# A gated linear attention with a max-out layer: one run of row-tiled products per unit, and two PSUM pairs that swap roles

## Chip, core and metric

The kernel runs on one core of one Trainium2 chip. The metric is the device time of the whole kernel in microseconds; the kernel before took 144.9 us (median of three runs, 144.42 to 144.99).

## The reference

Two stages, with B = 4 batches, H = 8 heads, S = 768 tokens, D = 48, a model width of 384 and 1024 hidden columns:

```python
# stage 1: a recurrence over the tokens, for each batch and head
for t in range(S):
    state = alpha[:, :, t, :, None] * state + np.einsum('bhd,bhe->bhde', k[:, :, t], v[:, :, t])
    y[:, :, t] = np.einsum('bhd,bhde->bhe', q[:, :, t], state)
# stage 2: on x = y as 3072 rows of H * D = 384
h1 = x @ w1
h2 = x @ w2
out = maximum(h1, h2) @ w_out
```

The kernel doesn't walk token by token. It takes chunks of 128 tokens, sums the logarithms of alpha along a chunk with matrix products, scales q and k by exponentials of those sums, and gets y as a masked product P = q k^T on v within the chunk plus q on the state at the chunk's start. The maximum is written as relu(x (w1 - w2)) + x w2, and the part that is linear in x uses w2 @ w_out, worked out once.

## The kernel before

A unit `u` is 256 tokens (two chunks, `cc` = 0 and 1) of one batch; there are NU = 12 units, in three rounds over the four batches (B = 4). In the step for `u` the attention of `u`, the max-out layer of `u - 1` and the beginning of `u + 1` are interleaved. The order of the statements is each engine's order of work (the schedule is a manual one), and every semaphore follows from which tiles an instruction reads and writes.

PSUM has eight banks here: `g0` to `g3` (one each), a pair `pp` and a pair `m`.

The pieces that matter, with cuts marked:

```python
def sumd(u):                       # decay sums of whole half chunks
    X = st[u]
    lg = X["lg"]
    cs = [new(f"g{i}", [128, 512], FP32, 1, "cs") for i in range(2)]
    X["csv"] = csv = [x[:, 0 : H * D]... for x in cs]          # cut
    X["dps"] = dps = cs[0][:, H * D : H * D + 4 * HP]...       # cut: other columns of the first bank
    for hp in range(HP):           # HP = 4 head pairs
        for j in range(2):
            nc.tensor.matmul(dps[:, hp], lhsT=pair(lg[:, j], hp), rhs=halves, ...)

def sumc(u):                       # running sums, one bank for each chunk; 64 rows each
    for j in range(2):
        for i in range(2):
            ...
                r = slice(64 * i, 64 * i + 64)
                m, x = mc[r, j], lg[r, j, :, 0:D]
            nc.tensor.matmul(csv[i], lhsT=m, rhs=x, start=(j == 0), stop=(j == 1))

def expm(u, cc):                   # ScalarE: Em = exp(-sum)
    nc.scalar.activation(out=Em, in_=X["csv"][cc], func=ACTF.Exp, scale=-1.0)
def expp(u, cc):                   # ScalarE: exp(sum), in place in PSUM
    nc.scalar.activation(out=X["csv"][cc], in_=X["csv"][cc], func=ACTF.Exp)
def expd(u):                       # ScalarE: de = exp(decay sums)
    nc.scalar.activation(out=X["de"], in_=X["dps"], func=ACTF.Exp)

def qmul(u, cc):                   # VectorE: qn = q * exp(sum)
    nc.vector.tensor_mul(out=X["qn"][cc][:, :, 0:D], in0=part(u, "qf", cc), in1=X["csv"][cc])

def kvmm(u, cc):                   # TensorE: k^T v of a chunk, into g3 or g2
    X["kvp", cc] = kvp = new(f"g{3 - cc}", [128, HP, 2 * D], FP32, 1, "kv")
    ...
def kvsum(u, cc): ...              # VectorE: tm = kv + scaled state, two instructions
def state(u, cc): ...              # GpSimd: sb = decayed state, from tm

def pmm(u, cc):                    # TensorE: P of a chunk; 48 rows, the two halves a at rows 0 and 64
    X["pa", cc] = pa = [new("pp", [128, HP, C], FP32, 2, "pp") for _ in range(2)]
    for j in range(HP):
        for a in range(2):
            r = slice(64 * a, 64 * a + D)
            nc.tensor.matmul(pa[a][:, j, :], lhsT=qk[r, 1, j, :], rhs=qk[r, 0, j, :], ...)
def pmask(u, cc, heads=(0, 1)): ...  # VectorE: pt = P * triangular mask, one instruction a half

def ystate(u):                     # TensorE: q on the state, begins Y; 48 rows
    X["ya"] = ya = [new(f"g{2 + a}", [128, 2, HP, D], FP32, 1, "ya") for a in range(2)]
    ...
def yin(u): ...                    # TensorE: pt on v, ends Y; ScalarE copies ya to xn
def xturn(u): ...                  # TensorE turns xn, into g2; VectorE copies to xt

def hid(u, f2, on_act=None, tag="m"):  # TensorE: six products; then relu on ScalarE or VectorE
    hp = new(tag, [128, 2, 2 * C], FP32, 2, "hp")
    ...
def outx(u, n): ...                # TensorE: three products into a new tile of "m"
def outg(u, n, ...): ...           # eight more onto it, then a copy on ScalarE
```

The step of the loop, for units 3 to 11 (the conditions of unit 2 are cut):

```python
for u in range(2, NU):
    nxt = u + 1 < NU
    ...
    kvmm(u, 0)
    pmm(u, 0)
    kvsum(u, 0)
    pmask(u, 0)
    state(u, 1)
    if more(u):                    # u + 4 < NU
        kvmm(u, 1)
    hid(u - 1, 0)
    hid(u - 1, 1)
    if nxt:
        sumd(u + 1)
    hid(u - 1, 2)
    if nxt:
        sumc(u + 1)
        expm(u + 1, 0)
        expp(u + 1, 0)
        expm(u + 1, 1)
    if more(u):
        kvsum(u, 1)
    pmm(u, 1)
    ystate(u)
    pmask(u, 1)
    hid(u - 1, 3, True)
    if nxt:
        expp(u + 1, 1)
        expd(u + 1)
        for cc in range(2):
            kmul(u + 1, cc)        # GpSimd: kn = k * Em
            qmul(u + 1, cc)
        state(u + 1, 0)
    outp(u - 1, 0)                 # outx and outg
    yin(u)
    if nxt:
        turn(u + 1, 0)             # kn and qn turned, into g0 and g1; VectorE copies to qk
        turn(u + 1, 1)
    outx(u - 1, 1)
    ...                            # xturn(u), v of u + 1, logarithms of u + 2, outg(u - 1, 1)
```

Of the kernel before, what the change touches and what calls it, by code (L numbers as in the profile page):

```python
# [9 lines left out]
FP32 = mybir.dt.float32  # L10
# [5 lines left out]
def kernel(  # L16
# [28 lines left out]
    B, H, S, D = q.shape  # L45
    C = 128
    HP = H // 2
    P64 = 64
    ND2 = S // (2 * C)
    NU = B * ND2  # L50
    NT, DM = out.shape
# [12 lines left out]
    nc.scalar.preload_act_table_set("natural_log_exp_and_others")  # L64

    st = {}

    def rows(src, u, lo, n):
        d, b = divmod(u, B)
        return src[b, :, d * 2 * C + lo : d * 2 * C + lo + n, :]  # L70
# [29 lines left out]
    def load(u):  # L100
        load_a(u)
        if u in PAIRED:
            load_fat(u, "kf", k)
            load_fat(u, "qf", q)
        else:
            load_kq(u, 0)
            load_kq(u, 1)
        load_v(u)
# [8 lines left out]
    for n in range(2):  # L117
        f = slice(n * NF // 2, (n + 1) * NF // 2)
# [4 lines left out]
    for n in range(4):  # L123
        f = slice(n * DFF // 4, (n + 1) * DFF // 4)
# [32 lines left out]
    for n in range(NB):  # L157
        t = constp.tile([128, 2, H, P64], FP16, name=f"lg{n}")
# [13 lines left out]
    for n in range(2 * NB):  # L172
        for lst, nm in ((QN, "qn"), (KN, "kn")):
            t = constp.tile([128, H, P64], FP16, name=f"{nm}{n}")
# [9 lines left out]
    def pair(t, j):  # L184
        return t[:, 2 * j : 2 * j + 2, :].rearrange("p h w -> p (h w)")

    def new(tag, shape, dtype, bufs, name):
        return psp.tile(shape, dtype, tag=tag, bufs=bufs, name=name)
# [21 lines left out]
                    nc.gpsimd.tensor_copy(out=X["v16"][64 * cc : 64 * cc + 64, 2], in_=i)  # L210

    def sums(u):
        sumd(u)
        sumc(u)

    def sumd(u):
        X = st[u]
        lg = X["lg"]
        cs = [new(f"g{i}", [128, 512], FP32, 1, "cs") for i in range(2)]
        X["csv"] = csv = [x[:, 0 : H * D].rearrange("p (h d) -> p h d", h=H) for x in cs]  # L220
        X["dps"] = dps = cs[0][:, H * D : H * D + 4 * HP].rearrange("p (j b n) -> p j b n", j=HP, b=2)
        for hp in range(HP):
            for j in range(2):
                nc.tensor.matmul(
                    dps[:, hp], lhsT=pair(lg[:, j], hp), rhs=halves, start=(j == 0), stop=(j == 1)
                )
# [100 lines left out]
    def kvsum(u, cc):  # L327
        X = st[u]
        tm = X[f"tm{cc}"] = gp.tile([128, HP, D], FP32, tag=f"tm{cc}", bufs=6 if cc else 3, name="tm")
        kvp = X["kvp", cc]  # L330
        for a in range(2):
            r = slice(64 * a, 64 * a + 64)
            e = slice(D * a, D * a + D)
            if ("sb", cc) in X:
                nc.vector.tensor_add(out=tm[r], in0=kvp[r, :, e], in1=X["sb", cc][r])  # L335
            else:
                nc.vector.tensor_copy(out=tm[r], in_=kvp[r, :, e])

    def more(u):
        return u + B < NU  # L340

    def pmm(u, cc):
        X = st[u]
        qk = X["qk"][:, cc].rearrange("p (n h) t -> p n h t", n=2)
        X["pa", cc] = pa = [new("pp", [128, HP, C], FP32, 2, "pp") for _ in range(2)]
        for j in range(HP):
            for a in range(2):
                r = slice(64 * a, 64 * a + D)
                nc.tensor.matmul(pa[a][:, j, :], lhsT=qk[r, 1, j, :], rhs=qk[r, 0, j, :], start=True, stop=True)  # L349

    def pmask(u, cc, heads=(0, 1)):
        X = st[u]
        if 0 in heads:
            X["pt", cc] = gp.tile([128, 2, HP, C], FP16, tag="pt", name="pt")
        pt = X["pt", cc]
        for a in heads:
            nc.vector.tensor_mul(  # L357
                out=pt[:, a], in0=X["pa", cc][a], in1=um.unsqueeze(1).to_broadcast([128, HP, C])
            )
# [4 lines left out]

    def ystate(u):
        X = st[u]
        X["ya"] = ya = [new(f"g{2 + a}", [128, 2, HP, D], FP32, 1, "ya") for a in range(2)]
        X["begun"] = begun = set()
        for cc in range(2):
            if ("sb", cc) not in X:  # L370
                continue
# [3 lines that stand above are left out]
                    nc.tensor.matmul(  # L375
                        ya[a][:, cc, j, :], lhsT=X["qk"][r, cc, j, :], rhs=X["sb", cc][r, j, :],
                        start=a not in begun, stop=False,
                    )
                    begun.add(a)
# [24 lines left out]
        X["xt"] = mp.tile([128, ND, 2, C], FP16, tag="xt", bufs=3, name="xt")  # L404
        nc.vector.tensor_copy(out=X["xt"], in_=xp)

    def hid(u, f2, on_act=None, tag="m"):
        X = st[u]
        if f2 == 0:
            X["gT"] = mp.tile([128, NF, 2 * C], FP16, tag="gT", name="gT")  # L410
        gT = X["gT"]
        hp = new(tag, [128, 2, 2 * C], FP32, 2, "hp")
        for n in range(2):
            f = 2 * f2 + n
            for ds in range(ND):
                nc.tensor.matmul(  # L416
                    hp[:, n, :], lhsT=w12[:, ds, f * 128 : (f + 1) * 128],
                    rhs=X["xt"][:, ds].rearrange("p n t -> p (n t)"), start=(ds == 0), stop=(ds == ND - 1),
                )
        if f2 != 3 if on_act is None else on_act:  # L420
            nc.scalar.activation(out=gT[:, 2 * f2 : 2 * f2 + 2, :], in_=hp, func=ACTF.Relu)  # L421
        else:
            nc.vector.tensor_relu(out=gT[:, 2 * f2 : 2 * f2 + 2, :], in_=hp)
# [5 lines left out]
    def outx(u, n):  # L429
        X = st[u]  # L430
        if n == 0:
            X["outs"] = mp.tile([128, 2, DM], FP32, tag="outs", bufs=4, name="outs")
        X["op"] = op = new("m", [128, DM], FP32, 2, "op")
        for ds in range(ND):
            nc.tensor.matmul(op, lhsT=X["xt"][:, ds, n, :], rhs=w2o[:, ds, :], start=(ds == 0), stop=False)  # L435

# [14 lines left out]
    def dst(u):  # L451
        d, b = divmod(u, B)
        t0 = b * S + d * 2 * C
        return out[t0 : t0 + 2 * C, :].rearrange("(p j) d -> p j d", j=2)

    def outlast(u, n):

        X = st[u]
        for e in range(2):
            c = slice(e * 2 * DM // 3, DM if e else 2 * DM // 3)  # L460
            op = new("m", [128, c.stop - c.start], FP32, 2, "oq")
            for ds in range(ND):
                nc.tensor.matmul(op, lhsT=X["xt"][:, ds, n, :], rhs=w2o[:, ds, c], start=(ds == 0), stop=False)
            for f in range(NF):
                nc.tensor.matmul(
                    op, lhsT=X["gT"][:, f, n * C : (n + 1) * C], rhs=wo16[:, f, c], start=False, stop=(f == NF - 1)
                )
            if e == 0:
                nc.scalar.copy(out=X["outs"][:, n, c], in_=op)
                nc.scalar.dma_start(out=dst(u)[:, n, c], in_=X["outs"][:, n, c])  # L470
            else:
                nc.vector.tensor_copy(out=X["outs"][:, n, c], in_=op)
                nc.sync.dma_start(out=dst(u)[:, n, c], in_=X["outs"][:, n, c])
# [141 lines left out]
    for u in range(2, NU):  # L615
        nxt = u + 1 < NU
        if u + 4 < NU:
            load(u + 4)
        if u == 2:
            pmm(u, 0)  # L620
            pmask(u, 0)
            hid(u - 1, 0)
        kvmm(u, 0)
        if u > 2:
            pmm(u, 0)
        kvsum(u, 0)
        if u > 2:
            pmask(u, 0)
        state(u, 1)
        if more(u):  # L630
            kvmm(u, 1)
        if u > 2:
            hid(u - 1, 0)
        hid(u - 1, 1)
        if nxt:
            sumd(u + 1)
        hid(u - 1, 2)
        if nxt:
            sumc(u + 1)
            expm(u + 1, 0)  # L640
            expp(u + 1, 0)
            expm(u + 1, 1)
        if more(u):
            kvsum(u, 1)
        pmm(u, 1)
        ystate(u)
        pmask(u, 1)
        hid(u - 1, 3, True)
        if nxt:
            expp(u + 1, 1)  # L650
            expd(u + 1)
            for cc in range(2):
                kmul(u + 1, cc)
                qmul(u + 1, cc)
            state(u + 1, 0)
        outp(u - 1, 0)
        yin(u)
        if nxt:
            turn(u + 1, 0)
# [3 lines that stand above are left out]
            xturn(u)  # L663
            vcast(u + 1)
            if u + 2 < NU:
                ln(u + 2)
            outg(u - 1, 1)
        else:
            outg(u - 1, 1, (0, 1, 2, 3))
            xturn(u)  # L670
            outg(u - 1, 1, (4, 5, 6, 7))
    for f2 in range(4):
        hid(NU - 1, f2, f2 % 2 == 0, "pp" if f2 % 2 else "m")
    outp(NU - 1, 0)
    outlast(NU - 1, 1)

# [28 lines left out]
```

## Time and profile before

| | before |
|---|---|
| time, median of three | 144.9 us |
| span of the profiled run | 142.9 us |
| hid's products (128x256), 288 | 37.6 us busy |
| products on w_out (128x384), 184 | 34.0 us busy |
| P (48 rows, 128 columns), 192 | 9.8 us busy, 217 ns each |
| sums of sumc on 64 rows (384 columns), 40 | 5.0 us busy |
| decay sums of sumd (4 columns), 96 | 4.2 us busy |
| Y's state part (48 rows, 48 columns), 160 | 4.0 us busy |
| relu on ScalarE (128x512), 46 | 27.4 us busy, 597 ns each |
| mask of P on VectorE (128x512), 48 | 31.0 us busy, 685 ns each |

How to read the profile: PE is TensorE's products, PEld its weight loads, DVE VectorE, ACT ScalarE, POOL GpSimd, SPq the queue that issues transfers. `L349` is a line of the kernel; `pp<-qk` says that a tile of that name is written from another; `48*128` is the weights' shape and `48x128` that of the moving operand. A product's duration is its latency and overlaps the next one's, so what a product costs in a stream is the distance between starts. In a timeline each line has the start in us from the span's start, the duration of the group, the engine, and the count; in square brackets stands the idle time of the engine ahead of it and what ended it.

### The profile page before, as it was taken

What the parts mean: (1) busy time and instruction counts of PE and PEld (TensorE: products, weight loads), DVE (VectorE), ACT (ScalarE), POOL (GpSimd) and SP (SyncE); (2) the same over time, 40 slices, a digit from 0 to 9 for tenths busy, and PEclk for the clock granted to TensorE, in tenths of its full rate; (3) what the DMA queues carried; (4) which work ended last, traced back from release to release, by engine and by line L of the source; (5) the groups of instructions that cost most, each with busy time, mean ns of one, the idle gap of its engine ahead of it and who ended that gap; (6) DMA issues with size and microseconds to landing.
All of it is one profiled execution on the core that took longest, in us unless ns stands there. A gap on an engine that the chain in (4) does not pass through costs nothing.

```text
span 142.9 us, 4263 instructions
## 1 busy us (share of the span) xinstructions
PE 134.8 (94%) x1687; PEld 96.7 (68%) x1687; DVE 88.3 (62%) x185; ACT 96.5 (68%) x201; POOL 56.9 (40%) x113
## 2 busy tenths in 40 slices
PE   6968879999999999999999999999999999999991
PEld 2335545655867767777877777678777776776771
DVE  6048857955976757766767677566676674762310
ACT  3467742498687688688786976786878768664321
POOL 7491452066345155172291371641813815410000
PEclk9999999999999999999999999999999999999999
DMA  4999999969999889998896897998979959020203
GB/s 106 271 363 337 312 339 348 262 120 197 222 136 262 146 223 234 173 221 152 251 193 124 264 207 128 320 155 225 253 126 293 193 93 381 36 110 5 95 15 110
DMA packets 76483, 28.58 MB, mean 200 GB/s; under 512 B 71728, under 2 KB 74672, under 8 KB 76464
## 3 DMA queue, kind: packets, MB, share of 16 engines
q1 hardware_dynamic: 76320, 28.19, 86.6%
q8 instruction: 13, 0.21, 0.7%
q10 hardware_dynamic: 144, 0.13, 0.3%
q14 instruction: 6, 0.05, 0.2%
HBM read 23.59 MB, written 4.72 MB: 198 GB/s over the span
## 4 chain that ended last, share of the span: by engine, by line
PE 70%; SPq 22%; DMA 4%; issue 1%; ACT 1%; DVE 0%
PE hp L416 21%; PE op L441 19%; SPq L75 10%; PE op L435 7%; PE tp L300 6%; SPq L85 5%; PE pp L349 4%; DMA af<-in_alpha_dram 4%; PE ya L387 3%; PE cs L238 3%; SPq L122 2%; SPq L125 2%; PE xp L403 2%; PE kv L322 2%; SPq L115 2%; PE ya L375 1%
## 5 line engine op out<-in xcount | busy, mean ns | idle before, releaser
L421 ACT ACTIVATE gT<-hp 128x512 f16<-128x512 f32 x46 | 27.4, 597 | 16.1 <-PE hp L416 15.6
L416 PE MATMUL hp<-xt,w 128*128 128x256 f16 x288 | 37.6, 273 | 0.4 <-DVE w L506 0.2
L357 DVE TENSOR_TENSOR pt<-pp,um 128x512 f16<-128x512 f32 x48 | 31.0, 685 | 9.1 <-PE pp L349 8.7
L441 PE MATMUL op<-wo,gT 128*128 128x384 f16 x184 | 34.0, 326 | 0.0
L286 POOL TENSOR_TENSOR kn<-kf,Em 128x384 f16<-128x384 f32 x24 | 23.4, 998 | 22.6 <-ACT Em L248 22.0
L416 PEld LDWEIGHTS <-w 128*128 128x128 f16 x288 | 25.7, 97 | 5.3 <-DVE w L506 0.7
L441 PEld LDWEIGHTS <-gT 128*128 128x128 f16 x184 | 17.5, 98 | 10.5
L278 POOL TENSOR_TENSOR sb<-tm,dd 128x192 f16<-128x192 f32 x20 | 10.1, 507 | 32.9 <-DVE tm L335 23.0
L290 DVE TENSOR_TENSOR qn<-qf,cs 128x384 f16<-128x384 f32 x24 | 12.3, 550 | 13.9 <-ACT de L258 13.0
L445 ACT COPY outs<-op 128x384 f32<-128x384 f32 x23 | 11.0, 479 | 13.1 <-PE op L441 12.8
L335 DVE TENSOR_TENSOR tm<-kv,sb 64x192 f32<-64x192 f32 x32 | 11.3, 353 | 9.4 <-PE kv L322 7.9
L307 DVE COPY qk<-tp 128x1024 f16<-128x1024 f16 x20 | 13.0, 686 | 4.4 <-PE tp L300 4.4
L206 POOL CAST v<-vf 64x384 f16<-64x384 f32 x24 | 12.0, 501 | 8.2 <-DMA vf<-in_v_dram 7.4
L435 PE MATMUL op<-w2o,xt 128*128 128x384 f16 x69 | 15.0, 326 | 0.0
L248 ACT ACTIVATE Em<-cs 128x384 f32<-128x384 f32 x24 | 11.7, 486 | 2.6 <-PE cs L238 2.6
L208 ACT CAST v<-vf 64x384 f16<-64x384 f32 x24 | 12.2, 510 | 1.6 <-DMA vf<-in_v_dram 1.1
L194 ACT ACTIVATE lg<-af 128x768 f16<-128x768 f32 x12 | 10.1, 843 | 4.1 <-DMA af<-in_alpha_dram 3.7
L253 ACT ACTIVATE cs<-cs 128x384 f32<-128x384 f32 x24 | 11.8, 493 | 0.0
L512 PE MATMUL warm<-wz 128*128 128x512 f16 x28 | 9.6, 461 | 1.3 <-DVE halves L150 1.3
L300 PE MATMUL tp<-ident,qn 128*128 128x128 f16 x96 | 9.3, 219 | 1.3 <-DVE qn L290 1.3
L394 ACT CAST xn<-ya 128x384 f16<-128x384 f32 x24 | 10.4, 490 | 0.1
L349 PE MATMUL pp<-qk 48*128 48x128 f16 x192 | 9.8, 217 | 0.4 <-DVE qk L305 0.4
(66 smaller groups left out, 156.8 us busy)
## 6 DMA issues: line engine op xcount, KB each, us to landing
af<-in_alpha_dram SPq DMA_DIRECT2D x12, 384.0 KB, 5.7
vf<-in_v_dram SPq DMA_DIRECT2D x12, 384.0 KB, 4.8
out_dram<-outs SPq DMA_DIRECT2D x11, 384.0 KB, 4.4
kf<-in_k_dram SPq DMA_DIRECT2D x40, 96.0 KB, 4.6
qf<-in_q_dram SPq DMA_DIRECT2D x40, 96.0 KB, 4.1
w2f<-in_moe_w_dram SPq DMA_DIRECT2D x3, 512.0 KB, 5.9
wof<-in_moe_w_out_dram SPq DMA_DIRECT2D x2, 768.0 KB, 9.3
w1f<-in_moe_w_dram SPq DMA_DIRECT2D x4, 384.0 KB, 8.1
```

What stands on the lines that cost most here:

```text
L75: nc.sync.dma_start(out=t[name].rearrange("p h j d -> p h (j d)"), in_=rows(src, u, 0, 2 * C).rearrange("h (p j) d -> p h (j d)", j=2),)
L208: nc.scalar.copy(out=o, in_=i)
L286: nc.gpsimd.tensor_mul(out=X["kn"][cc][:, :, 0:D], in0=part(u, "kf", cc), in1=X["Em"][cc])
L290: nc.vector.tensor_mul(out=X["qn"][cc][:, :, 0:D], in0=part(u, "qf", cc), in1=X["csv"][cc])
L300: nc.tensor.transpose(tp[:, n, j, :], pair(src, j), ident)
L307: nc.vector.tensor_copy(out=X["qk"][:, cc], in_=tp.rearrange("p n h t -> p (n h) t"))
L349: nc.tensor.matmul(pa[a][:, j, :], lhsT=qk[r, 1, j, :], rhs=qk[r, 0, j, :], start=True, stop=True)
L357: nc.vector.tensor_mul(out=pt[:, a], in0=X["pa", cc][a], in1=um.unsqueeze(1).to_broadcast([128, HP, C]))
L416: nc.tensor.matmul(hp[:, n, :], lhsT=w12[:, ds, f * 128 : (f + 1) * 128], rhs=X["xt"][:, ds].rearrange("p n t -> p (n t)"), start=(ds == 0 ...
L421: nc.scalar.activation(out=gT[:, 2 * f2 : 2 * f2 + 2, :], in_=hp, func=ACTF.Relu)
L435: nc.tensor.matmul(op, lhsT=X["xt"][:, ds, n, :], rhs=w2o[:, ds, :], start=(ds == 0), stop=False)
L441: nc.tensor.matmul(op, lhsT=X["gT"][:, f, n * C : (n + 1) * C], rhs=wo16[:, f, :], start=False, stop=(f == NF - 1))
```

## The change

From unit 3 on, P of chunk 0 leaves its place between the products of the two chunks' kv and stands ahead of the sums of the next unit; P of both chunks, these sums and Y's state part, all of which are on 48 or 64 rows, so follow each other in one run. Its purpose is that TensorE changes less often between products on all rows and products on half of them.

To have the banks for it, P of chunk 0 goes into the pair that the max-out layer doesn't hold, P of chunk 1 into `g3` and `g2`, and Y's state part into the pair that hid 1 and hid 2 have just used; then the two pairs swap roles, and hid 3 and what follows it take the other pair. The decay sums are split: head pairs 0 and 1 stay ahead of hid 2, head pairs 2 and 3 come after the run, ahead of hid 3. kvsum of chunk 1 moves up, behind hid 1. The split and kvsum's new place hold for unit 2 too.

```diff
+    moe, alt = ["m"], ["pp"]
...
+    def sumb(u):
+        X = st[u]
         cs = [new(f"g{i}", [128, 512], FP32, 1, "cs") for i in range(2)]
         X["csv"] = csv = [...]
-        X["dps"] = dps = cs[0][:, H * D : H * D + 4 * HP]...
-        for hp in range(HP):
+        X["dps"] = cs[0][:, H * D : H * D + 4 * HP]...
+
+    def sumd(u, hps=tuple(range(HP))):
+        lg, dps = st[u]["lg"], st[u]["dps"]
+        for hp in hps:
...
-    def pmm(u, cc):
+    def pmm(u, cc, tags=("pp", "pp")):
...
-        X["pa", cc] = pa = [new("pp", [128, HP, C], FP32, 2, "pp") for _ in range(2)]
+        X["pa", cc] = pa = [
+            new(t, [128, HP, C], FP32, 1 if t[0] == "g" else 2, "pp") for t in tags
+        ]
...
-        X["ya"] = ya = [new(f"g{2 + a}", [128, 2, HP, D], FP32, 1, "ya") for a in range(2)]
+        if u > 2:
+            ya = [new(moe[0], [128, 2, HP, D], FP32, 2, "ya") for a in range(2)]
+        else:
+            ya = [new(f"g{2 + a}", [128, 2, HP, D], FP32, 1, "ya") for a in range(2)]
+        X["ya"] = ya
...     (hid, outx and outlast: new(moe[0], ...) in place of new("m", ...))
         kvmm(u, 0)
-        if u > 2:
-            pmm(u, 0)
         kvsum(u, 0)
-        if u > 2:
-            pmask(u, 0)
         state(u, 1)
         if more(u):
             kvmm(u, 1)
         if u > 2:
             hid(u - 1, 0)
         hid(u - 1, 1)
+        if more(u):
+            kvsum(u, 1)
         if nxt:
-            sumd(u + 1)
+            sumb(u + 1)
+            sumd(u + 1, (0, 1))
         hid(u - 1, 2)
+        if u > 2:
+            pmm(u, 0, (alt[0], alt[0]))
+            pmask(u, 0)
         if nxt:
             sumc(u + 1)
             expm(u + 1, 0)
             expp(u + 1, 0)
             expm(u + 1, 1)
-        if more(u):
-            kvsum(u, 1)
-        pmm(u, 1)
+        if u > 2:
+            pmm(u, 1, ("g3", "g2"))
+        else:
+            pmm(u, 1)
         ystate(u)
         pmask(u, 1)
+        if u > 2:
+            moe[0], alt[0] = alt[0], moe[0]
+        if nxt:
+            sumd(u + 1, (2, 3))
         hid(u - 1, 3, True)
```

More of the change, by code (lines that the diff above doesn't have):

```diff
@@ L212, in sums @@
     def sums(u):
+        sumb(u)
         sumd(u)
         sumc(u)
-    def sumd(u):
+    def sumb(u):
         X = st[u]
-        lg = X["lg"]
         cs = [new(f"g{i}", [128, 512], FP32, 1, "cs") for i in range(2)]
         X["csv"] = csv = [x[:, 0 : H * D].rearrange("p (h d) -> p h d", h=H) for x in cs]
-        X["dps"] = dps = cs[0][:, H * D : H * D + 4 * HP].rearrange("p (j b n) -> p j b n", j=HP, b=2)
-        for hp in range(HP):
+        X["dps"] = cs[0][:, H * D : H * D + 4 * HP].rearrange("p (j b n) -> p j b n", j=HP, b=2)
+    def sumd(u, hps=tuple(range(HP))):
+        lg, dps = st[u]["lg"], st[u]["dps"]
+        for hp in hps:
             for j in range(2):
@@ L405, in xturn, with hid @@
         nc.vector.tensor_copy(out=X["xt"], in_=xp)
-    def hid(u, f2, on_act=None, tag="m"):
+    def hid(u, f2, on_act=None, tag=None):
         X = st[u]
@@ L411, in hid @@
         gT = X["gT"]
-        hp = new(tag, [128, 2, 2 * C], FP32, 2, "hp")
+        hp = new(tag or moe[0], [128, 2, 2 * C], FP32, 2, "hp")
         for n in range(2):
@@ L432, in outx @@
             X["outs"] = mp.tile([128, 2, DM], FP32, tag="outs", bufs=4, name="outs")
-        X["op"] = op = new("m", [128, DM], FP32, 2, "op")
+        X["op"] = op = new(moe[0], [128, DM], FP32, 2, "op")
         for ds in range(ND):
@@ L460, in outlast @@
             c = slice(e * 2 * DM // 3, DM if e else 2 * DM // 3)
-            op = new("m", [128, c.stop - c.start], FP32, 2, "oq")
+            op = new(moe[0], [128, c.stop - c.start], FP32, 2, "oq")
             for ds in range(ND):
@@ L672 @@
     for f2 in range(4):
-        hid(NU - 1, f2, f2 % 2 == 0, "pp" if f2 % 2 else "m")
+        hid(NU - 1, f2, f2 % 2 == 0, alt[0] if f2 % 2 else moe[0])
     outp(NU - 1, 0)
```

## The prediction

> **What bounds the kernel now.** I read the page first (busy shares, slices, the chain that ended last), then the waits, then the timeline of each engine in one steady unit, u = 7, that starts at 86.47 us. From the page:
>
> ```profile
> PE 134.8 (94%) x1687; PEld 96.7 (68%) x1687; DVE 88.3 (62%) x185; ACT 96.5 (68%) x201; POOL 56.9 (40%) x113
> ...
> PE 70%; SPq 22%; DMA 4%; issue 1%; ACT 1%; DVE 0%
> ```
>
> TensorE is busy 94% of the span. The 22% of SPq on the chain are the loads of the first 33 us; from 39.9 us to the last products the chain in order of time is TensorE, but for some 0.05 us. So from unit 2 on, every nanosecond that TensorE's queue gains or loses is a nanosecond of the end. The starts of its groups in unit 7, from its timeline (start, duration, group, count):
>
> ```profile
> 86.47 0.33 PE L322 MATMUL kv<-v,kn 128*128 128x96 f16 x4
> 86.74 0.40 PE L349 MATMUL pp<-qk 48*128 48x128 f16 x8
> 87.07 0.34 PE L322 MATMUL kv<-v,kn 128*128 128x96 f16 x4
> 87.25 1.47 PE L416 MATMUL hp<-xt,w 128*128 128x256 f16 x12
> 88.56 0.34 PE L224 MATMUL cs<-halves,lg 128*128 128x4 f16 x8
> 88.76 0.81 PE L416 MATMUL hp<-xt,w 128*128 128x256 f16 x6
> 89.51 0.50 PE L238 MATMUL cs<-lg,mc 64*128 64x384 f16 x4
> 89.84 0.39 PE L349 MATMUL pp<-qk 48*128 48x128 f16 x8
> 90.07 0.36 PE L375 MATMUL ya<-sb,qk 48*128 48x48 f16 x16
> 90.37 0.83 PE L416 MATMUL hp<-xt,w 128*128 128x256 f16 x6
> ```
>
> Durations overlap, so a group's cost is the distance to the next start. Nowhere in this unit does TensorE wait. But two places cost more than their products. Products on half the rows (48*128, 64*128: the row-tiled ones) run two at a time: eight of P take 0.23 us (89.84 to 90.07) where the next group is row-tiled too. Around P of chunk 0 it is different: four kv take 0.18 us before hp (87.07 to 87.25) but 0.27 before pp, and pp takes 0.33 before kv. So entering a row-tiled run costs about 0.09 us and leaving it 0.10. The second run shows the same: six hp take 0.75 us before cs instead of 6 x 0.109 (12 hp in 88.56 - 87.25 = 1.31), again 0.10. Inside the run, sums to P takes 0.33 us for two pairs of 384 columns: no switch there.
>
> The other engine that matters is ScalarE in the same unit:
>
> ```profile
> 89.61 0.60 ACT L421 ACTIVATE gT<-hp 128x512 f16<-128x512 f32 x1 [0.26 <-PE hp L416]
> 90.11 0.48 ACT L248 ACTIVATE Em<-cs 128x384 f32<-128x384 f32 x1
> 90.49 0.49 ACT L253 ACTIVATE cs<-cs 128x384 f32<-128x384 f32 x1
> 90.90 0.48 ACT L248 ACTIVATE Em<-cs 128x384 f32<-128x384 f32 x1
> 91.27 0.59 ACT L421 ACTIVATE gT<-hp 128x512 f16<-128x512 f32 x1
> 91.74 0.50 ACT L253 ACTIVATE cs<-cs 128x384 f32<-128x384 f32 x1
> 92.15 0.20 ACT L258 ACTIVATE de<-cs 128x16 f32<-128x16 f32 x1
> ```
>
> The exponentials of chunk 0 (Em at 90.11, then cs in place at 90.49, done at 90.98) end 1.47 us after the sums began (89.51), and TensorE has then long been at hid 3 (90.37). And from VectorE's timeline:
>
> ```profile
> 92.38 0.56 DVE L290 TENSOR_TENSOR qn<-qf,cs 128x384 f16<-128x384 f32 x1 [0.82 <-ACT de L258]
> ```
>
> This small line decides my prediction. qmul of chunk 0 reads only csv[0], which was final at 90.98. Yet VectorE sat idle 0.82 us and started 0.03 us after `de` ended. `de` reads dps: other columns of the same PSUM tile cs[0], hence of the same bank. In all, the listing of this line has 11 such waits, 13.0 us. So two engines on one bank of one tile are ordered here even when they touch different columns, and even when both only read.
>
> **What the Trainium skill says.** "TensorEngine Tiling (Array Packing)", section Tiling Modes, Key Properties: changing the tiling mode drains TensorE. The trace agrees: 0.09 to 0.10 us per change. "PSUM — Partial Sum Buffer", section "PSUM bank collisions raise a hardware error": two engines may not be on the same bank and quadrant at once, different columns or not, reads included, and PSUM is to be guarded by bank, not by address. The wait of qn on de is such a guard. "TensorE: Matmul & The Clock Gate", Part 3 (Packing small matmuls): matmuls start and end in program order, so a waiting product holds all behind it. In unit 7 the starts do follow the program's order.
>
> **The change part by part, units 3 to 11.**
> - P of chunk 0 leaves its place between the two kv groups and joins the run sums, P of chunk 1, Y's state part. Removed: one entry (0.09) and one exit (0.10 to 0.11, the first product after it is also 0.01 longer). Gain 0.2 us a unit, 9 units: 1.8 us. The eight products themselves only move.
> - P of chunk 0 (0.22 us) now stands ahead of the sums, so the exponentials start that much later relative to hid 2's end; relative to the unit's start they come earlier.
> - kvsum(u, 1) moves ahead of P's mask on VectorE, so the g2/g3 banks that P of chunk 1 now uses are free in time: sb ends at 88.29, two of 0.36 follow, done 2.6 us after the unit's start; P of chunk 1 comes at about 3.05.
> - Y's state part goes into the pair of hid 1 and hid 2. It needs hid 2's relu: about 0.31 after hid 2's last product starts, plus 0.60, 0.91 in all. In the new run Y's part comes 0.20 + 0.22 + 0.33 + 0.23 = 0.98 after that product. Just free, at most 0.05 lost.
> - hid 3 takes the bank of P of chunk 0, half a. Its mask (0.69 each, from about 0.67) ends at 1.36 on the same clock; hid 3 would come at 0.98 + 0.19 + 0.11 = 1.28, or 1.38 with the moved decay sums before it. About 0.05 at worst.
> - **The decay sums of head pairs 2 and 3 (sumd) move from before hid 2 to after Y's state part.** Four products of 25 ns (eight take 0.20 us, 88.56 to 88.76): no cost in themselves. But they write dps in the bank of cs[0], and by then ScalarE has Em and the in-place exponential of csv[0] ahead of them in program order. By the guard just seen, TensorE must wait for the second of these.
>
> The size of that wait, from the start S of the sums. The sums of csv[0] end at about S + 0.17 + 0.32 = S + 0.49; Em starts 0.04 later, as relu does after hid (in the kernel before it started at S + 0.60, behind the relu); the next exponential follows 0.38 later and takes 0.49: S + 1.40. Waits of TensorE on ScalarE end some 0.05 after the releaser: S + 1.45. TensorE arrives there at S + 0.33 + 0.23 + 0.19 + 0.11 = S + 0.86. So it idles 0.59 us, in each unit that has a next one. This falls on the bound engine, with no other products to fill it, and hid 3, relu and all that follows move with it.
>
> Sum: units 3 to 10, 8 x (0.59 - 0.20) = +3.1 us. Unit 2 has the split sumd but no merged run: there the sums begin at 40.63, the exponential ends at 42.10 and hid 3 began at 41.66, so hid 3 comes at 42.15 + 0.10, +0.6. Unit 11 has no next unit: -0.2. Together **+3.5 us: 144.9 to 148.4 us, 2.4% slower.** ScalarE, VectorE and the turns further on move with TensorE and keep the slack they have: qmul is still released by de (about 0.37 later, less than TensorE's delay), the turns wait for nothing new.
>
> **Rivals.**
> - *No wait at the moved sumd* (its four columns are disjoint from csv[0]). Then the gain stands, less 0.1 a unit at hid 3: about 143 to 143.5, within 2%. For it speaks only that the split looks made to fill hid 3's wait for the mask; against it the 11 waits of qn on de, where not even a write is involved.
> - *The buffers become the bound*: P's mask behind kvsum on VectorE, or relu of hid 2 ahead of Y's state part. The sums above leave 0 to 0.1 us a unit, under 1 us in all. Where the sumd wait exists this is hidden beneath it; alone it gives some 144.
> - *The wait is longer*: if Em stays behind the relu as before (S + 0.60), the wait is 0.66: 149.0. If the wait is for all of ScalarE's work issued so far (the second Em too, 0.41 later), about 1.0 a unit: near 152. Against that: kn starts at 90.67, 0.07 after the Em it needs, while the next exponential still runs.
>
> **Range and chances.** The wait I hold for very likely, its size for known to 0.1 us a unit, or 0.9 us in all, besides half a microsecond between runs (144.42 to 144.99). The range 147.0 to 149.6 leaves the rivals outside. The 2% limit lies at 147.8, 0.6 under my figure, so a wait shorter by 0.07 us a unit would already fall within 2%: slower 0.77, same 0.21, faster 0.02.
>
> **What the changed profile would show.** TensorE's idle time before the L224 products grows by some 4 us (less in the listing than start to start, since modelled ends reach into the gap), released by ACT cs, once a unit from 2 to 10. The gap between Y's state part and the next start is about 0.7 us instead of 0.30. kv to kv shrinks from 0.60 to 0.18 us, and the P groups sit at 0.22 to 0.23. The unit's period in the steady part grows from 9.76 to about 10.15 us. I am wrong if the second half of sumd starts within 0.15 us of Y's last product, or if its releaser is VectorE or the relu.

## Result and the profile after

The changed kernel takes 150.25 us (median of six) where the kernel before takes 144.69 us in the same comparison. The ratios, here and below, leave out executions more than 1.5% above the fastest of their kernel (two of these six, at 151.8 and 151.9 us, and in the third experiment the profiled one, at 155.75 us). The ratio is 1.0362 (on the mean 149.96 us to 144.72), 95% interval 1.0331 to 1.0393, so 3.6% slower. The forecast was 148.4 us, 2.4% slower, with a range of 147.0 to 149.6. The direction was right; the size was too small.

Busy shares and the chain that ended last, from the page of the changed kernel:

```profile
PE 134.3 (91%) x1687; PEld 97.7 (66%) x1687; DVE 88.0 (59%) x185; ACT 98.3 (66%) x201; POOL 57.3 (39%) x113
...
PE 66%; SPq 21%; ACT 4%; DMA 4%; issue 3%; DVE 1%
```

TensorE has no more to do than before (134.3 us against 134.8), but the span is 148.2 us instead of 142.9, and ScalarE's part of the chain rose from 1% to 4%. TensorE now waits for ScalarE. TensorE's own list of waits names the place (total us, times, longest):

```profile
PE cs L230 <- ACT cs L259: 5.4, 9, 0.7
```

L230 is the decay sums (`sumd`), L259 the in-place exponential (`expp`); nine times, once in each of units 2 to 10. The timeline of TensorE in unit 7, which starts at 89.48 us here (start, duration, group, count; idle time ahead and what ended it in brackets):

```profile
89.48 0.50 PE L328 MATMUL kv<-v,kn 128*128 128x96 f16 x8
89.82 1.47 PE L428 MATMUL hp<-xt,w 128*128 128x256 f16 x12
91.13 0.24 PE L230 MATMUL cs<-halves,lg 128*128 128x4 f16 x4
91.33 0.82 PE L428 MATMUL hp<-xt,w 128*128 128x256 f16 x6
92.08 0.40 PE L357 MATMUL pp<-qk 48*128 48x128 f16 x8
92.31 0.49 PE L244 MATMUL cs<-lg,mc 64*128 64x384 f16 x4
92.64 0.39 PE L357 MATMUL pp<-qk 48*128 48x128 f16 x8
92.86 0.36 PE L387 MATMUL ya<-sb,qk 48*128 48x48 f16 x16
93.82 0.24 PE L230 MATMUL cs<-halves,lg 128*128 128x4 f16 x4 [0.59 <-ACT cs L259]
93.92 0.81 PE L428 MATMUL hp<-xt,w 128*128 128x256 f16 x6
```

The merged run does what it was built for: the eight kv products reach hid in 0.34 us, where kv, P and kv took 0.78 before, and P takes 0.23 us in its new place: 0.21 us less in all. But from Y's state part to the next product lie 0.96 us, where 0.30 lay before. Against the same listing of before, hid 3 starts 4.44 us after the unit's start instead of 3.90. ScalarE meanwhile:

```profile
92.18 0.60 ACT L433 ACTIVATE gT<-hp 128x512 f16<-128x512 f32 x1 [0.25 <-PE hp L428]
92.89 0.49 ACT L254 ACTIVATE Em<-cs 128x384 f32<-128x384 f32 x1
93.28 0.48 ACT L259 ACTIVATE cs<-cs 128x384 f32<-128x384 f32 x1
93.69 0.48 ACT L254 ACTIVATE Em<-cs 128x384 f32<-128x384 f32 x1
```

The exponential of chunk 0 ends at 93.77 us and the decay sums start at 93.82, 0.05 later.

### The profile page after: what moved, and what is told of

Its sections match the earlier page's. It is cut to its first block, busy times and chain, and to the rows that moved or that the text cites. A ratio compares the mean times of both kernels' runs of the same rounds, so it can differ in the third digit from the quotient of the medians.

```text
span 148.2 us, 4264 instructions
## 1 busy us (share of the span) xinstructions
PE 134.3 (91%) x1687; PEld 97.7 (66%) x1687; DVE 88.0 (59%) x185; ACT 98.3 (66%) x201; POOL 57.3 (39%) x113
## 4 chain that ended last, share of the span: by engine, by line
PE 66%; SPq 21%; ACT 4%; DMA 4%; issue 3%; DVE 1%
PE hp L428 20%; PE op L453 18%; SPq L78 10%; PE op L447 7%; PE tp L306 5%; SPq L88 5%; DMA af<-in_alpha_dram 4%; PE pp L357 3%; ACT cs L259 3%; PE ya L399 3%; SPq L125 2%; SPq L128 2%; PE xp L415 2%; PE cs L244 2%; PE cs L230 2%
## 5 line engine op out<-in xcount | busy, mean ns | idle before, releaser
L365 DVE TENSOR_TENSOR pt<-pp,um 128x512 f16<-128x512 f32 x48 | 30.2, 683 | 10.3 <-PE pp L357 10.3
L428 PEld LDWEIGHTS <-w 128*128 128x128 f16 x288 | 26.5, 97 | 4.8 <-DVE w L518 0.7
L259 ACT ACTIVATE cs<-cs 128x384 f32<-128x384 f32 x24 | 11.7, 486 | 0.0
L230 PE MATMUL cs<-halves,lg 128*128 128x4 f16 x96 | 5.4, 165 | 6.0 <-ACT cs L259 5.4
L230 PEld LDWEIGHTS <-lg 128*128 128x128 f16 x96 | 5.1, 97 | 8.1 <-issue 5.2
```

The costliest lines, as they stand in the source:

```text
L365: nc.vector.tensor_mul(out=pt[:, a], in0=X["pa", cc][a], in1=um.unsqueeze(1).to_broadcast([128, HP, C]))
L428: nc.tensor.matmul(hp[:, n, :], lhsT=w12[:, ds, f * 128 : (f + 1) * 128], rhs=X["xt"][:, ds].rearrange("p n t -> p (n t)"), start=(ds == 0 ...
```

## Experiments

All ratios are against the kernel before, run on the same chip. "Steady unit" is the distance between two starts of the first kv group, in units 4 to 7: 9.77 us before, 10.29 us in the changed kernel. In units 8 to 10, which have no second kv, it is 9.59 and 10.12.

### Undo the split alone

```diff
-            sumd(u + 1, (0, 1))        # ahead of hid 2
+            sumd(u + 1)
...
-        if nxt:
-            sumd(u + 1, (2, 3))        # ahead of hid 3
```

> The changed kernel with one part undone: all eight decay sums stand ahead of hid 2 again; the merged run and the pairs that swap roles stay. Theory A (the moved half of sumd waits for the exponential that holds its PSUM bank): no wait of TensorE on ScalarE's cs is left. In unit 7 of the changed kernel Y's state part ended its issue at 93.05 and hid 3 could start at 93.15, or when the mask's first half frees its bank, 92.51 + 0.69 + 0.05 = 93.25; it started at 93.92. So a steady unit falls from 10.29 to about 9.63 us, 0.14 under the kernel before; over 8 units -1.1, unit 11 keeps its +0.2: about 143.8 us, ratio 0.994. Theory B (the new places in PSUM, the mask behind kvsum and the swapped pairs, hold TensorE up): most of the loss stays, 148 us or more, ratio over 1.02.

Measured: 144.43 us, ratio 0.9956 (0.9932 to 0.9981); the steady unit is 9.63 us, as forecast. TensorE has no wait for ScalarE's cs left. From its timeline, unit 7 (start 86.89):

```profile
88.54 0.34 PE L230 MATMUL cs<-halves,lg 128*128 128x4 f16 x8
88.74 0.81 PE L428 MATMUL hp<-xt,w 128*128 128x256 f16 x6
89.49 0.40 PE L357 MATMUL pp<-qk 48*128 48x128 f16 x8
89.72 0.49 PE L244 MATMUL cs<-lg,mc 64*128 64x384 f16 x4
90.05 0.39 PE L357 MATMUL pp<-qk 48*128 48x128 f16 x8
90.28 0.36 PE L387 MATMUL ya<-sb,qk 48*128 48x48 f16 x16
90.67 0.82 PE L428 MATMUL hp<-xt,w 128*128 128x256 f16 x6
```

So theory A holds and B falls: the new banks, the swap and the mask's new place together cost no more than the merged run gains. Two things are to be seen in the lines. Hid 2 starts 1.85 us after the unit's start with eight decay sums ahead of it, just as it does in the changed kernel with four. And Y's state part to hid 3 takes 0.39 us instead of the 0.30 of before: the mask of P starts at 89.92 and its first half takes 0.69, so the bank that hid 3 needs is free at 90.61, and hid 3 starts 0.06 later. That last reading rests on the coincidence of the times, which comes again in the last unit (below, in the sixth experiment); no run takes this wait away.

### The split alone, on the kernel before

```diff
-            sumd(u + 1)
+            sumb(u + 1)
+            sumd(u + 1, (0, 1))
...
         pmask(u, 1)
+        if nxt:
+            sumd(u + 1, (2, 3))
         hid(u - 1, 3, True)
```

> The kernel before with one part of the change alone: the decay sums of head pairs 2 and 3 stand behind Y's state part, nothing else is moved. Theory A: TensorE waits there for the in-place exponential of chunk 0. From the start S of the sums: Em at S + 0.60, the next exponential 0.38 later for 0.49, 0.05 to TensorE, 0.10 for the four products: hid 3 at S + 1.62 instead of S + 0.86, +0.76 us in each of units 2 to 10: 144.7 + 6.9 = 151.6 us, ratio 1.047, more than the whole change costs. Theory B: with no bank moved and no mask displaced there is nothing to wait for: 144.7 us, ratio 1.00.

Measured: 151.4 us, ratio 1.0451 (1.0414 to 1.0488), steady unit 10.50 us. TensorE's timeline:

```profile
93.22 0.50 PE L241 MATMUL cs<-lg,mc 64*128 64x384 f16 x4
93.55 0.39 PE L352 MATMUL pp<-qk 48*128 48x128 f16 x8
93.78 0.36 PE L378 MATMUL ya<-sb,qk 48*128 48x48 f16 x16
94.74 0.24 PE L227 MATMUL cs<-halves,lg 128*128 128x4 f16 x4 [0.60 <-ACT cs L256]
94.84 0.38 PE L419 MATMUL hp<-xt,w 128*128 128x256 f16 x2
```

Hid 3 comes 1.62 us after the sums, as forecast. The split of sumd by itself costs more than the whole change does; the merged run gives part of it back.

### The decay sums in the other chunk's bank

```diff
-        X["dps"] = cs[0][:, H * D : H * D + 4 * HP]...
+        X["dps"] = cs[1][:, H * D : H * D + 4 * HP]...
```

> The changed kernel with one size of the guard changed: the decay sums' columns lie in the bank of the sums of chunk 1 instead of chunk 0, same place in the order. Theory A, that the bank counts and not the data: TensorE now waits for the last reader of that bank ahead of it, Em of chunk 1, which ended at 94.17 in unit 7 where the exponential of chunk 0 ended at 93.77: hid 3 0.40 later, 9 units, +3.6 us against the changed kernel: 153.5 us, ratio 1.061; the releaser is Em. Also qmul of chunk 0 no longer waits for de on VectorE, and qmul of chunk 1 does. Theory C (TensorE waits for the values of chunk 0's exponential, or for ScalarE in general at that point): unchanged at 149.9, ratio 1.036, releaser cs.

Measured: 154.11 us, ratio 1.0616 (1.0571 to 1.0661), steady unit 10.70 us. Of the profile only distances within a unit are used. TensorE's timeline:

```profile
97.05 0.36 PE L387 MATMUL ya<-sb,qk 48*128 48x48 f16 x16
98.41 0.24 PE L230 MATMUL cs<-halves,lg 128*128 128x4 f16 x4 [1.00 <-ACT Em L254]
```

and VectorE's, with both qmul of that unit:

```profile
99.09 0.54 DVE L296 TENSOR_TENSOR qn<-qf,cs 128x384 f16<-128x384 f32 x1
100.65 0.55 DVE L296 TENSOR_TENSOR qn<-qf,cs 128x384 f16<-128x384 f32 x1 [1.01 <-ACT de L264]
```

From Y's state part to the decay sums it is now 1.36 us instead of 0.96, 0.40 more, and the releaser is Em. The same products with the same data wait for another instruction, because their columns lie in another bank. And qmul of chunk 0 starts without a wait while qmul of chunk 1 now waits for de: the read-after-read guard that the prediction took from one line moved along with the bank. Theory C falls.

Two limits of this: the waits are those of the program's semaphores, and every PSUM tile of this kernel has a bank to itself. So the runs show that the order goes by bank or tile and not by columns or data; they do not separate the bank from the tile.

### The in-place exponential behind the moved sumd

```diff
             expm(u + 1, 0)
-            expp(u + 1, 0)
             expm(u + 1, 1)
...
             sumd(u + 1, (2, 3))
+            expp(u + 1, 0)
```

> The changed kernel with the in-place exponential of chunk 0 issued behind the moved half of sumd (ScalarE then does Em 0, Em 1, exponential 0). Theory A: only Em of chunk 0 is ahead of sumd on its bank; it ended at 93.385 in unit 7, 0.38 before the exponential. TensorE resumes 0.38 us earlier in each of 9 units, -3.4 us against the changed kernel: 146.5 us, ratio 1.013, steady unit about 9.91 us; the releaser is Em. Theory C (it waits for ScalarE's exponentials whatever their bank): unchanged, 149.9 us.

Measured: 146.96 us, ratio 1.0144 (1.0105 to 1.0184), steady unit 9.91 us. TensorE's timeline:

```profile
91.63 0.36 PE L387 MATMUL ya<-sb,qk 48*128 48x48 f16 x16
92.21 0.24 PE L230 MATMUL cs<-halves,lg 128*128 128x4 f16 x4 [0.21 <-ACT Em L254]
92.31 0.49 PE L428 MATMUL hp<-xt,w 128*128 128x256 f16 x3
```

The gap shrinks from 0.96 to 0.58 us, by the one instruction that no longer stands ahead on that bank. What is ahead on the bank in program order sets the wait, to the instruction.

### Half of sumd behind hid 2, where no exponential stands

The split alone again, on the kernel before, but with the second half between hid 2 and the sums:

```diff
-            sumd(u + 1)
+            sumb(u + 1)
+            sumd(u + 1, (0, 1))
...
         hid(u - 1, 2)
         if nxt:
+            sumd(u + 1, (2, 3))
             sumc(u + 1)
```

> The kernel before with the decay sums of head pairs 2 and 3 moved only from before hid 2 to behind it, ahead of the sums, so that no exponential stands between. Theory D (hid 2 waits for the bank that hid 0's relu frees, and the eight decay sums just filled that wait, so four of them leave 0.09 us of it open): hid 2 starts at the same time as before, the four products cost 0.10 us behind it, a steady unit grows from 9.77 to 9.86 us and the kernel by 9 x 0.10 = 0.9 us: ratio 1.006. Theory E (there is no such wait, the products only change places): steady unit 9.77 us, ratio 1.000. Under neither does TensorE wait for ScalarE's cs.

Measured: ratio 1.0038 (1.0021 to 1.0054), steady unit 9.83 us. TensorE's timeline, unit 7 (start 87.50):

```profile
89.59 0.24 PE L227 MATMUL cs<-halves,lg 128*128 128x4 f16 x4
89.78 0.81 PE L419 MATMUL hp<-xt,w 128*128 128x256 f16 x6
90.43 0.24 PE L227 MATMUL cs<-halves,lg 128*128 128x4 f16 x4
90.61 0.50 PE L241 MATMUL cs<-lg,mc 64*128 64x384 f16 x4
```

Hid 2 starts 2.28 us after the unit's start; in the kernel before it was 2.29, behind twice as many decay sums. Four of them take 0.19 us up to hid 2, as eight did (0.20). So it isn't the decay sums that set hid 2's start. Theory D says that it is relu of hid 0, which frees the bank that hid 2 takes: here this relu ends at 89.73 and hid 2 starts at 89.78, and in the changed kernel it ends at 91.28 and hid 2 starts at 91.33.

Two units in which the times fall otherwise bear this out. In unit 2 of the changed kernel the logarithm holds relu up, and TensorE's timeline lists the wait ahead of hid 2 and what ended it:

```profile
40.10 0.82 PE L428 MATMUL hp<-xt,w 128*128 128x256 f16 x6 [0.23 <-ACT gT L433]
```

In unit 10 of the fourth experiment hid 1 came late, so relu of hid 0 had long ended when the decay sums came (ScalarE's and TensorE's timelines):

```profile
118.83 0.60 ACT L433 ACTIVATE gT<-hp 128x512 f16<-128x512 f32 x1
119.64 0.24 PE L230 MATMUL cs<-halves,lg 128*128 128x4 f16 x4
119.74 0.81 PE L428 MATMUL hp<-xt,w 128*128 128x256 f16 x6
```

That relu ends at 119.43, and the four decay sums take 0.10 us up to hid 2 instead of 0.19.

The cost behind hid 2 was 0.08 us (hid 2 to the sums 0.83 instead of 0.75), a little less than the 0.10 expected, and the steady unit grew by 0.07 us (9.765 to 9.833) instead of 0.09. The ratio lies between the forecasts of theory D (1.006) and theory E (1.000), and its interval takes in neither; the lines speak for D.

### Whole sumd, and the last unit as before

On top of the first experiment, unit 11 is left as in the kernel before:

```diff
-        if u > 2:
+        if u > 2 and nxt:       # merged run, g3/g2 for P, swap of roles
...
+        if not nxt:             # unit 11: P of chunk 0 right after kv
+            pmm(u, 0, (alt[0], alt[0]))
```

> The changed kernel with all eight decay sums ahead of hid 2, and with unit 11 as in the kernel before (P of chunk 0 ahead of hid, Y's state part in g2 and g3, no swap). Expected: steady units of 9.63 and 9.46 us as with the whole sumd alone (9.77 and 9.59 before), and the part from unit 11 to the end 17.9 instead of 18.1 us: 8 x 0.13 = 1.0 us under the kernel before, about 143.8 us, ratio 0.993, unless the loads of alpha hold up a unit, as they did once in the run with the whole sumd (one unit of 10.37 us). If the time of unit 11 came from something other than the merged run, the last part stays at 18.1 us and the ratio near 0.995.

Measured: 144.16 us against 144.75, ratio 0.9953 (0.9933 to 0.9973); steady units 9.63 and 9.46 us; from unit 11's start to the end 17.88 us instead of 18.09 in the changed kernel, as in the kernel before (17.89). So unit 11's loss comes from the merged run in it; in the ratio it can't be told from the first experiment (0.9956). In the changed kernel that unit reads (timelines of TensorE, ScalarE and VectorE):

```profile
132.56 0.62 PE L357 MATMUL pp<-qk 48*128 48x128 f16 x16
133.01 0.65 PE L387 MATMUL ya<-sb,qk 48*128 48x48 f16 x16
133.73 0.82 PE L428 MATMUL hp<-xt,w 128*128 128x256 f16 x6
```

```profile
132.66 0.60 ACT L433 ACTIVATE gT<-hp 128x512 f16<-128x512 f32 x1 [0.25 <-PE hp L428]
```

```profile
132.99 2.48 DVE L365 TENSOR_TENSOR pt<-pp,um 128x512 f16<-128x512 f32 x4 [1.69 <-PE pp L357]
```

There is no next unit, hence no sums (0.33 us) between the two P, and what follows comes 0.33 us earlier at banks that are still in use. Relu of hid 2 ends at 133.26, and Y's state part, which needs its bank, lasts 0.65 us instead of 0.36. The first half of the mask, 0.69 us from 132.99, ends at 133.68, and hid 3, which takes that bank, starts 0.05 later. From Y's state part to hid 3 it is 0.72 us instead of 0.29; by these times the mask is the wait that ends last.

This version is 0.5% under the kernel before, where 8 x 0.13 us would be 0.7%. In the profiled executions the early units account for it: unit 3 took 9.99 us here (9.66 before), and in the first experiment unit 4 took 10.37. There ScalarE, and behind it TensorE, stood as follows (ScalarE's and TensorE's timelines of the first experiment):

```profile
57.72 0.84 ACT L197 ACTIVATE lg<-af 128x768 f16<-128x768 f32 x1 [1.38 <-DMA af<-in_alpha_dram]
```

```profile
58.99 0.81 PE L428 MATMUL hp<-xt,w 128*128 128x256 f16 x6 [0.58 <-ACT outs L457]
```

The logarithm waits for alpha; the copy of the output behind it comes late; hid 1 waits for the bank that this copy frees.

### Alpha's loads one unit ahead

```diff
     def load(u):
-        load_a(u)
+        if u < 4:
+            load_a(u)
+        elif u == 4:
+            load_a(4)
+            load_a(5)
+        elif u + 1 < NU and u > 4:
+            load_a(u + 1)
```

> The version with the whole sumd and unit 11 as before, with alpha's loads one unit further ahead in the queue (alpha of unit 5 with unit 4's load, then alpha of u + 5 with the rest of u + 4). In that version ScalarE waited for alpha after 40 us twice, 1.2 us in all (0.2 in the kernel before), and unit 3 took 9.99 us, unit 2 15.96. Theory F (it is the place of alpha in the queue of loads): no such wait after 40 us, unit 3 at 9.65 to 9.7 and no unit over it, ratio 0.992. Theory G (the loads as a whole are late there, the queue being full): another tensor's load is waited for instead, of v or of q and k, and the ratio stays at 0.995 or goes up.

Measured: ratio 0.9972 (0.9952 to 0.9993), no better. Unit 3 took 9.63 us, as theory F says, but units 4 to 6 took 10.17, 9.93 and 9.90 us, and units 9 and 10 took 9.90 and 9.75 instead of 9.46. The waits of ScalarE and of GpSimd from 33 us on (two lists):

```profile
ACT v L217 <- DMA vf<-in_v_dram: 4.7, 7, 1.2
ACT lg L203 <- DMA af<-in_alpha_dram: 1.0, 2, 0.7
```

```profile
POOL v L215 <- DMA vf<-in_v_dram: 13.0, 10, 2.1
```

ScalarE now waits 4.7 us for v where it waited 0.4 in the version before this, and still 1.0 us for alpha, where it was 1.8; GpSimd's waits for v went from 3.1 to 13.0 us. That is theory G: moving one tensor forward moved the wait to another. Why the loads are late stays open. It isn't only that a TensorE faster than 9.77 us a unit runs into them: in the fourth experiment, with a steady unit of 9.91 us, ScalarE waited 2.9 us for alpha from 33 us on, and units 3 and 10 took 10.26 and 10.16 us instead of 9.91 and 9.74. A run with smaller loads wasn't made.

## Why the prediction came out as it did

**What bounds the kernel.** Right for the changed kernel: TensorE's work is unchanged, and the time grew by what its queue waited. In later runs single units also waited for loads.

**The wait at the moved decay sums.** Right, with place, releaser, count and cause: nine waits, released by ScalarE's cs, set by what lies in the bank. The line of qn behind de was enough to see it, and the third and fourth experiments moved the wait by 0.40 and 0.38 us as the rule demands. The rival without a wait is out.

**The gain of the merged run.** Right: 0.2 us a unit was said. With whole sumd a steady unit gains 0.13 (9.765 to 9.633), after 0.09 lost at hid 3, which by the times goes to the mask; that makes 0.22. The prediction allowed 0.05 "at worst" for that mask wait.

**Where the sum was too small.** By its own terms, on the spans (142.91 to 148.22 us, +5.31):

| | predicted | measured |
|---|---|---|
| units 3 to 10, start to start | 8 x 0.39 = +3.1 | 77.49 to 81.81 us: +4.32 |
| unit 2 | +0.6 | 15.96 to 16.69: +0.73 |
| unit 11 to the end | -0.2 | 17.89 to 18.09: +0.20 |
| ahead of unit 2 | 0 | +0.06 |

- *"Four products of 25 ns ...: no cost in themselves."* This step failed, and it is the largest of three mis-sized terms. It took for granted that hid 2 comes 0.10 us earlier once four decay sums no longer stand ahead of it. It came at 1.85 us after the unit's start instead of 0.34 + 1.31 + 0.10 = 1.75, because the eight had just filled the wait for hid 0's relu: in the kernel before, that relu ends at 88.70 and hid 2 starts at 88.76. From "nowhere in this unit does TensorE wait" the prediction took it that hid 2 would follow its queue alone, while a wait stood there that other products filled. About 0.10 us a unit, 0.8 in all. The fifth experiment shows it by itself.
- *"Em starts 0.04 later, as relu does after hid (in the kernel before it started at S + 0.60, behind the relu)."* The relu wasn't the reason. In the changed kernel ScalarE had been free for 0.11 us (92.78 to 92.89), and Em still came at S + 0.58 (92.31 to 92.89). The exponential ended at S + 1.46 instead of S + 1.40. The larger figure stood among the rivals, for the wrong reason. 0.06 us a unit, 0.5 in all.
- *"Gain 0.2 us a unit, 9 units"*, unit 11 among them. The 0.98 us that made the bank of Y's state part "just free", and hid 3's bank nearly so, held the sums' 0.33 us, which unit 11 does not have. The term was -0.2 and measured +0.2, and the sixth experiment takes it back by undoing the merged run there.
- Unit 2 is right in its mechanism: from its first decay sums (39.62) to hid 3 (42.47) it takes 2.85 us instead of 2.26 (39.40 to 41.66), +0.59. The remaining 0.14 lie ahead of those sums, where the logarithm waits for alpha's load.

The three mis-sized terms make 0.8 + 0.5 + 0.4 = 1.7 us of the 1.8 us that the span gained beyond the forecast of 3.5. The rest nearly cancels: a steady unit lost 0.52 us and not 0.39 + 0.10 + 0.06 = 0.55, while unit 3, unit 2 and the part ahead of it lost 0.1 us each or a little less beyond their terms.

Two sums don't come out of the prediction's own terms. The rival without a wait, whose gain stands "less 0.1 a unit", gives 144.9 - 1.8 + 0.9 = 144.0 us and not 143 to 143.5; the first experiment, without the wait, took 144.43. And the gap from Y's state part to the next start follows as 0.30 + 0.59 = 0.89 us, not 0.7; it measured 0.96.

The range failed because it was built on a spread of 0.1 us in one wait, as if every other term were known. Two of the three terms above are banks that came free just in time, and the third is the start of one exponential.

## What to carry to other kernels

When a small product is moved within TensorE's queue, look up what shares its PSUM bank (here the same as its tile), not only what it reads. Here it waited for the last instruction ahead of it on that bank (moved by +0.40 and -0.38 us with that instruction), and even two readers were ordered (0.82 us). A stretch without waits can hide one that other products fill, so before taking work out of it compare each buffer's release with the start of its next user. And a gain of 1% can be lost in single units that wait for loads (0.3 to 0.7 us in one unit here); look at the units one by one.

## What was not expected of the hardware

- ScalarE's Em starts 0.10 us after the modelled end of the row-tiled sums (92.80 to 92.89), while relu starts 0.04 us after hid's. Why was not tried.
- Four decay sums set between hid 2 and the row-tiled sums cost 0.08 us where four of 25 ns would be 0.10: part of them may lie within the change of tiling, which takes 0.10 us in any case. No run separates the two.
